# One more channel slice of a long convolution inverted by an eight-way split, with the pacing of the work lengthened

## The chip, the cores and the metric

The kernel runs on one core of one Trainium2 chip. The metric is device time in microseconds (us). It computes the output and all gradients of one layer, so it has ten outputs. Engines are named as in the profile: PE is TensorE (matrix products), DVE is VectorE, ACT is ScalarE, POOL is GpSimd and SP is SyncE, which here only issues transfers. PEld is the loading of the stationary operand of a matrix product.

## The reference

With S = 2048 rows, D = 1024 channels and F = 3584 hidden columns, the layer computes

```
xn = layernorm(x)
kv = shift_conv4(k) * v                       # four taps along the rows
y  = irfft(rfft(kv, 2S) * rfft(ssm_k, 2S))[:S] + kv * ssm_D
s  = xn * y                                   # long convolution branch
h  = (xn @ w_gate) * (xn @ w_up)
g  = silu(h @ w_down)                         # gated linear branch
out = x + s * g
```

and then the gradients of `out` to x, k, v, the shift taps, `ssm_k`, `ssm_D`, `w_gate`, `w_up` and `w_down`, for a given `grad_out`. The change concerns only how `y` is brought back from the frequency domain for some of its channels.

## The kernel before

The channels of the long convolution are done in eight slices of 128 channels, ds = 0 to 7 (the sixth slice is ds = 5). Each slice is transformed to 16 groups of spectra on 128 partitions, with 256 columns (two halves of the rows for 128 channels). For a slice the order is: forward transform of the filter and of `kv` (lines 771 to 796), product of the spectra (333 to 358), inverse (line 847), and after that its rows (`tail`, 743 to 752). The inverse has a VectorE part that leaves a tile G of 16 groups (a tile named HX in the trace), and a TensorE part, four row groups `rp`, each of which writes one PSUM tile `psY`, is copied to `yf` by ScalarE, and after the fourth is stored to DRAM as `YFd`.

There are two versions of this inverse, and the tuple `INV8` (line 680) says which slices use the second.

- `inv_dft` (367 to 388) and `inv_rows` (441 to 452): the VectorE part stops after two levels of sums and differences, six instructions. Each row residue then needs four matrix products of 128x256, so a slice needs 32.
- `inv8` (395 to 430) and `inv8_rows` (433 to 439): the VectorE part goes one level further, 16 instructions, some of them with the factor C8. Each residue needs two matrix products, so a slice needs 16.

While the convolution runs on VectorE, TensorE does the gate and up products: 14 column slabs of 256 by 16 row blocks, each block eight matrix products 128x512 into `psg` (line 645). After each block a function `tick` counts one and lets the convolution, a Python generator, emit more instructions. Each `yield` carries a weight in us; `F_TOTAL` (859 to 861) is the sum of the weights, and each tick lets the generator go on until its done weight reaches

```
(SHIFT_W + (F_TOTAL - SHIFT_W) * (cnt[0] + 6.5) / (NT + 3.5))        # line 923, NT at line 916
```

where `cnt` is the tick's number. The weights are of VectorE time less 0.95 of the TensorE time that the convolution adds (`net`, line 244). A tick is a quarter of a unit: a unit is one call of `gu_unit`, four row blocks of one slab. The VectorE multiplication that makes `hN` of a unit (line 659) is emitted at the next unit's first block, and is transposed on TensorE five blocks later (line 674).

After the last block (cnt = 195) comes the down product of the gated branch, in pairs of row blocks: a pair is 28 column chunks of four matrix products 128x512 into two PSUM tiles `psbm` (line 968), so 112 for a pair. The first pair (`bm_first`) still ticks, after every second chunk, so that cnt ends at 209. Then `drain` (line 1260) emits what is left of the convolution, PSUM and SBUF rooms of the convolution are given back, and from there the seven other pairs follow, each block with its `gate` (1197 to 1235): ScalarE copies `psbm` to `bm`, and VectorE computes output and gradients of the gate from `bm`, `x_t`, `do_t`, `xn_t` and `yf_t`. The last is read from `YFd`, all slices at once. The three PSUM accumulators of this phase (`psbm`: two in `ps_bm`, one in `ps_bx`) come free with the copy to `bm`, and the third and fourth blocks of the phase use `ps_bx` and then the first block's own accumulator again.

The instructions of an engine are put in order at build time by a planner with its own model of durations: of the instructions that its model holds to be ready it takes the one that stands first in the program. VectorE instructions of the convolution are pinned in program order (lines 207 to 213); matrix products of the rows (line 438 and 449) are not. In the finished program every engine runs its list strictly in order.

Of the kernel before, what the change touches and what calls it, by code (L numbers as in the profile page):

```python
# [19 lines left out]
def build_kernel(  # L20
# [433 lines left out]
    def by_res(t, rp):  # L454

        return t.rearrange("p (c r) d -> p r c d", c=2)[:, 2 * rp:2 * rp + 2]

    def rowps(ps):
        return ps[:].rearrange("p r (c d) -> p r c d", c=2)
# [217 lines left out]

    h_out = []
    EIGHT = ((0, 0), (0, 1), (7, 0), (7, 1))
    INV8 = (2, 4, 6, 7)  # L680
    SHIFT_W = 8 * 2.3

    conv_state = {"forward": True, "filters": True}
# [1 line left out]
    def conv_forward():  # L685
# [54 lines left out]
        def kvs(ds):  # L740
            return S_["kvt", ds // 2][:, :, ds % 2 * P:(ds % 2 + 1) * P]

        def tail(ds):
            G = S_.pop(("G", ds))
            yf = cs.tile([P, NB, P], BF16, name="yf")
            for rp in range(4):
                ps = (inv8_rows if ds in INV8 else inv_rows)(G, ps_y, rp)
                pe_us[0] += 0.45 if ds in INV8 else 0.9
                nc.scalar.copy(out=by_res(yf[:], rp), in_=rowps(ps))
# [14 lines left out]
        def half(ds, x, i, first=None):  # L764
            if (ds, int(first is not None)) not in EIGHT:
                return fwd4_half(x, i, cf, ps_cv, first)
            SP = cf.tile([P, 2, 2, 512], F32, name="SP", bufs=2)
            fwd8_half(x, i, SP, ps_cv, first, True)
            return SP
# [36 lines left out]
        for ds in range(8):  # L806
# [37 lines left out]
            def ahead():  # L844
                if ds < 7:
                    sp.append(half(ds + 1, kvs(ds + 1), len(sp)))
            yield from (inv8 if ds in INV8 else inv_dft)(KX, HX, cs, ahead if ds % 2 == 0 else None, ahead)
            if ds % 2 == 1:
# [11 lines left out]
    F_TOTAL += len(EIGHT) * (FWD8_W - 9.6 + 0.95 * 1.75) - 2.0  # L860
    F_TOTAL += len(INV8) * (INV8_W - INV_W + 0.95 * 1.8)
    conv = conv_forward()
# [50 lines left out]
    ps_cv = pool("ps_cv", 2, space=PSUM)  # L913
    pump, drain = make_pump(conv, F_TOTAL)
    cnt = [-5]
    NT = 24 * 8.0 + 20

    def tick(by=1):
        cnt[0] += by
# [2 lines left out]
        if cnt[0] >= -2:  # L922
            pump((SHIFT_W + (F_TOTAL - SHIFT_W) * (cnt[0] + 6.5) / (NT + 3.5)) / F_TOTAL)

# [648 lines left out]
def kernel(  # L1573
# [22 lines left out]
    out_9: bass.AP,  # L1596
):
    build_kernel(
        ctx, tc,
        A_q, A_k, A_v, A_shift_k, A_ssm_k, A_ssm_D, B_x, B_w_gate, B_w_up, B_w_down, grad_out,  # L1600
# [32 lines left out]
```

## Time and profile before

| | us |
|---|---|
| median of three runs (1922.61 to 1923.16) | 1922.94 |
| the profiled execution's own time | 1922.53 |
| span of the profiled execution, first to last instruction | 1920.8 |
| gate and up products, roughly | 9 to 513 |
| first pair of the down product | 513 to 539 |
| other seven pairs | 539 to 711 |
| PE busy in the span | 1902.7 |
| DVE busy in the span | 1548.5 |

The profile lists each engine's busy time; windows of it give busy time for a stretch, and the timeline gives instructions in order, with equal neighbours merged (an "x4" at the end is four instructions) and, in brackets, the idle time before them and what ended it. The chain of waits is what led to the last instruction, followed backwards; the list of waits says which engine sat idle for whom. Matrix products overlap in the records: one of 128x256 is shown as 272 ns long, while eight in a row take 0.87 us.

### The profile page before, as it was taken

How to read it: one execution, taken by the hardware profiler on the slowest of the kernel's cores; microseconds unless marked ns; L12 is line 12 of the kernel's file. 1: busy time of each engine (PE TensorE's matmuls, PEld its weight loads, DVE VectorE, ACT ScalarE, POOL GpSimd, SP SyncE). 2: the span in 40 equal slices, each digit the busy share in tenths (PEclk: the TensorE clock that was granted, in tenths of full speed). 3: DMA queues.
4: the chain of work that ended last, by engine and by line, in shares of the span. 5: the costliest groups of instructions: out<-in, count | busy, mean ns of one | idle time of the engine just before them, and what ended most of it. 6: DMA issues, size and time to landing. Idle time of an engine off the chain costs nothing.

```text
span 1920.8 us, 27294 instructions
## 1 busy us (share of the span) xinstructions
PE 1902.7 (99%) x10828; PEld 1028.9 (54%) x10962; DVE 1548.5 (81%) x1705; ACT 638.9 (33%) x943; POOL 328.7 (17%) x461
## 2 busy tenths in 40 slices
PE   8999999999999999999999999999999999999999
PEld 5555655555444456666666666664444444444444
DVE  8999999999967555887899999999996404288884
ACT  5754655555332233332222222221212102011113
POOL 5121212201112220001031131111212001011111
PEclk9999999999999999999999999999999999999999
DMA  8776867659799988557788698585786999889885
GB/s 297 266 262 218 261 208 233 219 207 295 256 295 318 296 305 242 202 196 239 240 255 266 220 259 263 196 283 166 231 255 168 140 207 222 161 176 195 196 177 167
DMA packets 451360, 444.43 MB, mean 231 GB/s; under 512 B 268800, under 2 KB 371612, under 8 KB 436768
## 3 DMA queue, kind: packets, MB, share of 16 engines
q1 hardware_dynamic: 394848, 243.36, 48.3%
q0 software_dynamic: 40064, 169.95, 27.7%
q10 hardware_dynamic: 16320, 29.36, 4.1%
q8 instruction: 86, 1.41, 0.3%
q14 instruction: 42, 0.34, 0.1%
HBM read 194.00 MB, written 185.64 MB: 198 GB/s over the span
## 4 chain that ended last, share of the span: by engine, by line
PE 82%; DVE 7%; issue 4%; DMA 4%; ACT 2%; SPq 0%; POOL 0%; DVEq 0%; ACTq 0%; POOLq 0%
PE psb L1341 20%; PE psg L645 19%; PE psb L1324 10%; PE psbm L968 10%; PE psb L1419 9%; PE psx L1471 6%; PE psF L235 3%; DVE dkp L1179 2%; DMA dkT<-DKSHd 1%; PE tr L674 1%; DVE dxn L213 1%; PE psY L438 1%; PE psY L1127 1%; DMA dkh<-DKSHd 1%; PE psx L1419 1%
## 5 line engine op out<-in xcount | busy, mean ns | idle before, releaser
L645 PE MATMUL psg<-wslab,U 128*128 128x512 bf16 x1734 | 401.7, 379 | 6.1 <-DMA wslab<-in_B_w_gate_dram 2.4
L1341 PE MATMUL psb<-U,U 128*128 128x512 bf16 x1792 | 397.1, 379 | 0.0
L1471 PE MATMUL psx<-U,dgut 128*128 128x512 bf16 x1505 | 331.0, 379 | 1.6
L1471 PEld LDWEIGHTS <-dgut 128*128 128x128 bf16 x1792 | 175.3, 98 | 211.4
L1341 PEld LDWEIGHTS <-U 128*128 128x128 bf16 x1792 | 175.2, 98 | 198.0
L645 PEld LDWEIGHTS <-U 128*128 128x128 bf16 x1792 | 172.4, 98 | 187.9 <-issue 2.5
L1324 PE MATMUL psb<-wdt,U 128*128 128x256 bf16 x1792 | 205.6, 273 | 0.0
L1324 PEld LDWEIGHTS <-U 128*128 128x128 bf16 x1792 | 175.3, 98 | 29.2
L213 DVE TENSOR_TENSOR W<-W 128x1024 f32<-128x1024 f32 (+1 forms) x180 | 177.7, 1004 | 3.9
L1419 PE MATMUL psb<-U,U 128*128 128x512 bf16 x797 | 175.9, 379 | 0.9
L1346 ACT CAST wb<-psb 128x512 bf16<-128x512 f32 x112 | 65.6, 586 | 315.4 <-PE psb L1341 313.4
L968 PE MATMUL psbm<-U,ht 128*128 128x512 bf16 x658 | 144.8, 379 | 0.7
L1419 PEld LDWEIGHTS <-U 128*128 128x128 bf16 x896 | 87.5, 98 | 104.5
L647 ACT CAST gut<-psg 128x512 bf16<-128x512 f32 x156 | 91.4, 587 | 123.7 <-PE psg L645 118.3
L1503 ACT ACTIVATE dx_t<-dxn 128x1024 bf16<-128x1024 f32 x15 | 15.9, 1057 | 326.9 <-DVE dxn L213 326.9
L1179 DVE SCALAR_TENSOR_TENSOR dkp<-dkT,kT 128x1024 bf16<-128x1024 bf16 (+2 forms) x64 | 78.4, 1224 | 41.1 <-DMA dkT<-DKSHd 39.4
L968 PEld LDWEIGHTS <-ht 128*128 128x128 bf16 x672 | 65.7, 98 | 78.6
L213 DVE TENSOR_TENSOR U<-U,dht 128x2048 bf16<-128x2048 bf16 x56 | 68.3, 1221 | 46.2 <-ACT dht L1326 46.1
L1326 ACT CAST dht<-psb 128x512 bf16<-128x512 f32 x112 | 65.6, 587 | 116.4 <-PE psb L1324 115.2
L66 POOL DMA_DIRECT2D Hd<-hN x54 | 36.7, 679 | 294.3 <-DVE hN L213 291.2
L213 DVE TENSOR_TENSOR dxn<-psx,dxna_t 128x1024 f32<-128x1024 f32 x15 | 18.3, 1222 | 77.1 <-PE psx L1471 73.1
L1450 ACT CAST wbs<-psb 128x512 bf16<-128x512 f32 x51 | 29.9, 586 | 145.1 <-PE psb L1419 131.2
(237 smaller groups left out, 2446.5 us busy)
## 6 DMA issues: line engine op xcount, KB each, us to landing
U<-GUd SPq DMA_DIRECT2D x28, 1024.0 KB, 7.2
DGd<-U SPq DMA_DIRECT2D x28, 1024.0 KB, 6.6
GUd<-gut ACTq DMA_DIRECT2D x39, 512.0 KB, 6.4
out_dram<-wb SPq DMA_DIRECT2D x112, 128.0 KB, 4.2
U<-Hd SPq DMA_DIRECT2D x14, 1024.0 KB, 6.5
Hd<-hN POOLq DMA_DIRECT2D x54, 256.0 KB, 4.3
HTd<-hT SPq DMA_DIRECT2D x52, 256.0 KB, 3.6
ht<-HTd SPq DMA_DIRECT2D x6, 1536.0 KB, 11.4
```

Of the source, the lines that this page charges most:

```text
L213: pinned(V.tensor_tensor(o, a, b, op))
L235: mm = nc.tensor.matmul(ps[:, k].rearrange("p (c d) -> p c d", c=2), T[:, r, k, :], xr[:, r], start=(n == 0), stop=(n == len(rs) - 1 and ( ...
L645: gu_mm[0] = nc.tensor.matmul(ps[:], XNT[q][:, dc, qi * P:(qi + 1) * P], w[:, dc].rearrange("p a f -> p (a f)"), start=(dc == 0), stop=(dc ...
L647: nc.scalar.copy(out=gut[:, :, i], in_=ps[:].rearrange("p (a f) -> p a f", a=2))
L968: mm = nc.tensor.matmul(ps[:, dh * 512:(dh + 1) * 512], ht(fc)[:, i * P:(i + 1) * P], WD[fc // 4][:, fc % 4, dh * 512:(dh + 1) * 512], sta ...
L1179: ins = V.scalar_tensor_tensor(prod[:].rearrange("p r d -> p (r d)")[:, lo:H], dkT[:, 0, lo:H], 1.0, kT[:, 0, 13 + m + lo:13 + m + H], op0 ...
L1324: nc.tensor.matmul(ps[:, x * SLW:(x + 1) * SLW], DBMT[2 * hf + g][:, dc, (b % 4) * P:(b % 4 + 1) * P], wdt[:, dc, :], start=(dc == 0), sto ...
L1326: nc.scalar.copy(out=dht[:, 2 * e:2 * e + 2].rearrange("p b f -> p (b f)"), in_=ps[:])
L1341: nc.tensor.matmul(ps[:], XN[b // 4][:, b % 4, dc * P:(dc + 1) * P], dgus[b // 8][:, :, b % 8], start=(b == 0), stop=(b == NB - 1))
L1346: nc.scalar.copy(out=wb[:, dc % 2].rearrange("p a f -> p (a f)"), in_=ps[:])
L1419: nc.tensor.matmul(ps, h[:, f, b, :], DBM[b // 4][:, b % 4, dh * 512:(dh + 1) * 512], start=(b == 0), stop=(b == NB - 1))
L1471: nc.tensor.matmul(ps[:, dh * 512:(dh + 1) * 512], t[n][:, f, i * P:(i + 1) * P], WGU[n][:, f, dh * 512:(dh + 1) * 512], start=(n == 0 and ...
```

## The change

The tuple `INV8` gains slice 5, so its inverse goes by `inv8` and `inv8_rows` where it went by `inv_dft` and `inv_rows`. `F_TOTAL` follows `len(INV8)`. `NT` is longer by five ticks, while the number of ticks that are really made is not changed.

```diff
-    INV8 = (2, 4, 6, 7)
+    INV8 = (2, 4, 5, 6, 7)
 ...
-    NT = 24 * 8.0 + 20
+    NT = 24 * 8.0 + 25
```

Where the tuple is used: line 747 (which row products), 748 (their TensorE weight, 0.45 for 0.9), 847 (which inverse) and 861 (the sum of weights).

## The prediction

> **What bounds the kernel now.** First the page's busy line, then windows, then who waited for whom. PE is busy for 1902.7 of 1920.8 us. In the stage of the convolution DVE is just as full (19.8 of 20 us), up to 535 us; then it has room. The list of waits of PE from 60 to 700 us has two entries of 0.2 us: nothing holds PE in that time.
>
> ```profile
> PE 1902.7 (99%) x10828; PEld 1028.9 (54%) x10962; DVE 1548.5 (81%) x1705; ACT 638.9 (33%) x943; POOL 328.7 (17%) x461
> ```
> ```profile
> 400.00:420.00 20.00, 19.89 (x119) 10.96 (x119) 19.83 (x13) 10.02 (x15) 1.90 (x3) 1.00 0.68 233
> ...
> 500.00:520.00 20.00, 19.87 (x115) 9.98 (x116) 19.76 (x23) 8.26 (x12) 3.58 (x5) 1.00 0.91 295
> 520.00:540.00 20.00, 19.89 (x96) 9.44 (x97) 15.55 (x16) 1.08 (x3) 0.00 (x0) 1.00 0.90 258
> 540.00:560.00 20.00, 19.89 (x96) 9.47 (x97) 9.94 (x17) 9.88 (x11) 3.68 (x5) 1.00 0.88 245
> ```
> ```profile
> PE psF L235 <- ACT SP L295: 0.2, 1, 0.2
> PE psF L235 <- ACT SP L257: 0.2, 1, 0.2
> ```
>
> (The windows' columns are stretch, length, PE, PEld, DVE, ACT, POOL, clock, DMA share, GB/s.) Now the places of the change: in the chain, a row group of the sixth slice (x8) and of the seventh (x4); in the timeline, the VectorE inverse of the sixth slice, then of the eighth, and what PE and DVE do after it.
>
> ```profile
> 431.85 0.87 PE psY L449 x8
> ...
> 488.07 0.44 PE psY L438 x4
> ```
> ```profile
> 410.83 2.28 DVE L213 TENSOR_TENSOR W<-KX 128x2048 f32<-128x2048 bf16 x1
> 413.03 0.69 DVE L213 TENSOR_TENSOR hN<-U 128x1024 bf16<-128x1024 bf16 x1
> 413.63 2.35 DVE L213 TENSOR_TENSOR HX<-W 128x1024 bf16<-128x1024 f32 x2
> ...
> 420.63 0.68 DVE L213 TENSOR_TENSOR hN<-gut 128x1024 bf16<-128x1024 bf16 x1
> ```
> ```profile
> 516.87 0.68 DVE L213 TENSOR_TENSOR hN<-gut 128x1024 bf16<-128x1024 bf16 x1
> ...
> 519.86 2.29 DVE L213 TENSOR_TENSOR W<-KX 128x2048 f32<-128x2048 bf16 x1
> ...
> 533.29 2.50 DVE L283 SCALAR_TENSOR_TENSOR HX<-W 128x512 bf16<-128x512 f32 x4
> 536.77 0.53 PEld L438 LDWEIGHTS <-TI 128*128 128x128 bf16 x4
> 537.31 1.50 PEld L968 LDWEIGHTS <-U 128*128 128x128 bf16 x8
> 538.93 0.53 PEld L438 LDWEIGHTS <-TI 128*128 128x128 bf16 x4
> 539.47 0.64 PEld L968 LDWEIGHTS <-U 128*128 128x128 bf16 x4
> ...
> 546.28 0.69 DVE L213 TENSOR_TENSOR gg<-bm,sig 128x1024 bf16<-128x1024 bf16 x1 [10.49 <-ACT sig L1211]
> ```
>
> The eighth slice's G is complete at 535.79. Its first row group runs 1 us later, after 104 of the first pair's 112 weight loads (16 and 5 and 83 in this view); DVE then stands idle for 10.49 us.
>
> **PE, removed.** Sixteen matrix products 128x256. A row group takes 0.87 us by `inv_rows` and 0.44 by `inv8_rows`; four groups: 4 x 0.43 = 1.7 us. PE waits for nothing here, so this lies on the path: -1.7 us. The copies to `yf` and the store of `YFd` stay as they are. [...]
>
> **DVE, added.** The sixth slice's inverse ran from 410.83 to 420.63, less one `hN` in between (0.60 from start to start): 9.20 us. The eighth slice's, by the longer version, ran undisturbed from 519.86 to 535.79: 15.93. So +6.73 us, on an engine that has no idle time until 535.8. All of the convolution behind it comes 6.7 us later on DVE, and the eighth G is complete at 535.79 + 6.73 = 542.5. What takes this up is the idle 10.49 us before the first gate, and the seven gates behind, which need some 6.8 us of DVE for 12.1 us of PE each.
>
> **The pace.** `F_TOTAL` is 413.5 and gains 6.8 + 0.95 x 1.8 = 8.5, so 422.0. Per tick that is (413.5 - 18.4) / 215.5 = 1.833 before and (422.0 - 18.4) / 220.5 = 1.830 after. So up to the sixth inverse nothing moves by more than a tick. Behind it everything is emitted 8.5 / 1.83, say five ticks later against PE's blocks: 5 x 1.73 us plus 1.25 transposes of `hN` at 0.45, less the 1.7 saved, 7.5 us. DVE moves by 6.7 plus 1.25 `hN` at 0.60, also 7.5. So DVE's small lag behind the emission (0.6 to 3.6 us) stays, and with it the absence of PE waits up to 511 us. Costs nothing; if the lag grew, PE would wait for it one for one.
>
> **The moved rows.** Ticks end at 209: the pump stops at 215.5 / 220.5 and leaves 5 x 1.83 = 9.2 weight units; the convolution ends with 1.5 (last piece of the inverse), 3.0 and four times 1.0. So this piece and all four row groups come out of `drain`, behind all 112 products of the first pair. Those end at 538.9 before; without 1.7 and without the row group that stood ahead (0.44) PE is there at 536.8. G comes at 542.5. If the planner knows that, it fills the 5.8 us with some 26 products of the second pair, as it did with four between the last row groups, and the wait is 0. If it thinks G ready at once, PE waits 5.8 us. The trace has no such place; the nearest rows are the two early waits of PE for a normalised row of DVE, 0.8 and 0.7 us after some 8 to 10 us of unbroken DVE work: the plan ran 7 to 10% ahead of DVE. The chain from the last `hN` to G is 27.8 us (12 of product, 15.9 of inverse): 1.9 to 2.8 us. I take the low side, 2.0 us, since those rows are of short instructions and this chain of long ones; ends 0 and 5.8.
>
> **Queues behind the rows.** The last row group ends near 547, not 542.2. ACT: the copy to `bm` of the first block came right behind the fourth `yf` copy (542.86), so now near 548.7; its accumulator is wanted when the fourth block begins, 536.8 + 12.1 + 1.7 = 550.6 or later: 1.9 us spare, so nothing. POOL stores `YFd` (then idle for 24.7 us; behind it only gate stores). SP waits for that store (5.0 us) with `yf_t`, and behind it are the second gate's loads and the fourth pair's left operand `ht`, issued at 551.5, now 557; it takes 12.8 us to land and is wanted near 585: 15 us spare. Gates 1 to 4 come 5 to 6 us later and catch up. POOL's `KFd`, `HFd` and filter loads move with DVE; they run a slice ahead.
>
> The sum, against the profiled 1922.53: -1.7 + 2.0 = +0.3. The median is 0.4 above that execution, so **1923.2 us**: no change that a measurement tells (a bound of 0.2%, 3.8 us).
>
> **The rivals.** *Full wait, slower.* Row group one stands straight behind the 112, PE waits for G until 542.5. For it: the product order is fixed at build time, and the plan was ahead of DVE in both early waits. Against: it filled the gaps between the last row groups rightly. Price -1.7 + 5.8 = +4.1, 1927.0; it turns the sign beyond 1.7 us of wait, and passes 0.2% beyond 5.5.
> *No wait.* The second pair fills the whole time: 1922.9 - 1.7 = 1921.2. For it: G's delay is plain arithmetic that a model with right durations sees; against: the same early waits.
> *DVE sets the end.* If gates or transposes of `hN` hung on DVE, its 6.7 us would come through: 1922.9 + 6.7 = 1929.6. For it 19.8 of 20 us; against: no PE wait for DVE, 10.49 us idle right behind.
> *Accumulators.* The spare 1.9 us at the first `bm` copy is used up, say by a planner that puts the rows 5 us too late: +3.1 - 1.7, 1924.3, more if the next copies follow late.
> *The change does less than it says:* too few units would be left for `drain`; then rows still stand inside the first pair, G is later than them, and PE waits as in the first rival.
>
> **How the numbers follow.** Part wait (1 to 3.5 us: 1922.2 to 1924.7) 0.42; no wait (under 1: 1921.2 to 1922.2) 0.22; full wait (1924.7 to 1927.0) 0.20, a third of it beyond 0.2%; DVE through 0.08; accumulators and replanned order behind them 0.04, to 1929; better than the saving (a stall of the crowded place near 425 us gone too) 0.04. The range 1920.6 to 1927.6 leaves out the DVE case, part of the last two: 0.15. Slower by over 0.2%: 0.07 + 0.08 + 0.04, 0.19; faster by over 0.2%: 0.04; the rest, 0.77, within.
>
> **What would show it.** `psY` of line 449 at 96, of line 438 at 80 in the forward part. DVE's sixth inverse near 16 us; the eighth ends near 542.5. All four last row groups behind 112 weight loads of line 968; the number in between and PE's idle time before the first tell the rivals apart. First `bm` copy near 549, `yf_t` near 558. PE's other stages shift by one constant. It is wrong if PE waits before 511 us, or if a wait of 2 us or more stands at a gate's accumulator.

## The result and the profile after

The changed kernel takes 1929.17 us (median of seven, 1927.59 to 1930.26); the kernel before, on the same chip, 1922.94. The ratio is 1.0028 with a 95% interval of 1.0019 to 1.0038: slower by 0.2 to 0.4%, against a forecast of no change. The profiled execution took 1929.12 us, 6.59 more than the one of before.

Where the 6.59 us lie was read by comparing, in the two traces, the start of the n-th weight load of the gate and up products and of the down product:

| place | after minus before, us |
|---|---|
| first gate and up product | +0.55 (+0.43 by 410 us) |
| 449 us, behind the sixth slice's rows | -1.29 |
| 482 us | +2.97 |
| 513 us, start of the down product | +4.82 |
| 557 us, behind the last rows | +6.55 |
| from there to the end | +6.55, constant |

So the saving is there in full (-1.72 from 410 to 449 us), then 6.11 are lost between 449 and 513 us, and 1.74 at the last rows. The +0.43 stands from the first product on, before any convolution: it is no part of the change. (The rise from 482 to 513 us is no loss of its own: the gate and up products stand in another order among the convolution's, and PE waits for nothing there.)

First the granted clock, by windows of the kernel after (columns: stretch, length, PE, PEld, DVE, ACT, POOL, clock, DMA share, GB/s):

```profile
450.00:460.00 10.00, 9.45 (x56) 4.73 (x55) 9.86 (x10) 3.63 (x6) 0.67 (x1) 1.00 1.08 353
470.00:475.00 5.00, 2.93 (x18) 1.60 (x17) 4.69 (x3) 0.34 (x1) 0.00 (x0) 1.00 0.82 285
475.00:480.00 5.00, 3.79 (x10) 1.37 (x10) 1.48 (x3) 3.69 (x6) 0.50 (x1) 0.66 0.67 188
540.00:560.00 20.00, 18.59 (x95) 9.04 (x93) 9.50 (x12) 7.55 (x9) 1.15 (x1) 1.00 0.78 206
```

and the same three crowded windows of the kernel before:

```profile
450.00:460.00 10.00, 9.95 (x57) 5.18 (x57) 9.86 (x10) 5.72 (x9) 0.67 (x1) 1.00 0.98 316
470.00:475.00 5.00, 4.95 (x25) 2.29 (x24) 4.96 (x7) 2.09 (x4) 0.67 (x1) 1.00 0.66 183
475.00:480.00 5.00, 5.00 (x40) 3.30 (x38) 4.97 (x7) 4.72 (x7) 0.67 (x1) 1.00 0.96 317
```

PE lost 2 us in 470 to 475, and in the next 5 us it ran ten products where 40, some of them shorter, ran before, at a granted clock of 0.66. ScalarE was busy for 0.34 of the 5 us from 470. The windows at 450 and 540 show the smaller losses: 9.45 of 10 us, and 18.59 of 20. The lists of waits of the kernel after, of PE from 60 to 720 us and of ScalarE from 430 to 520 us (total, times, longest), name the two places and their cause:

```profile
PE psg L645 <- ACT gut L647: 4.1, 2, 3.3
PE psY L438 <- DVE HX L283: 1.3, 1, 1.3
```
```profile
ACT hT L675 <- DMA HTd<-hT: 5.9, 1, 5.9
ACT gut L647 <- DMA GUd<-gut: 3.4, 1, 3.4
```

The last line belongs to the smaller loss at 459 us: a store of `gut` that landed after 10.6 us (8.0 in the kernel before). ScalarE's wait for the store of `hT` was 0.75 us in the kernel before:

```profile
470.76 1.01 ACT L675 COPY hT<-tr 128x1024 bf16<-128x1024 bf16 x1 [0.75 <-DMA HTd<-hT]
```

The timeline of the kernel after shows the chain in order: ScalarE's copy to `hT` cannot start until an older `hT` has been stored; the copy of `psg` to `gut` is queued behind it; PE has no free `psg` until then; and when PE goes on, its weight loads are 0.43 us apart (0.15 + 0.28) where they are 0.216 elsewhere.

```profile
474.66 1.01 ACT L675 COPY hT<-tr 128x1024 bf16<-128x1024 bf16 x1 [5.88 <-DMA HTd<-hT]
475.57 0.59 ACT L647 CAST gut<-psg 128x512 bf16<-128x512 f32 x1
...
476.21 5.30 PE L645 MATMUL psg<-wslab,U 128*128 128x512 bf16 x16 [3.28 <-ACT gut L647]
...
476.99 0.15 PEld L645 LDWEIGHTS <-U 128*128 128x128 bf16 x1 [0.28 <-issue]
```

The distances between weight loads give the size: one of 0.99 us (459.23) and one of 3.66 (472.55) where 0.22 is normal, and behind the second seven of 0.43 between one of 0.35 and one of 0.29, which are 1.7 us more than nine of 0.216: 0.77 + 3.44 + 1.7 = 5.9 of the 6.1 us.

The store came late because of what was queued then. This is the issue of transfers by SP and by POOL, after

```profile
448.22 0.37 SPq L540 DMA_DIRECT2D wslab<-in_B_w_up_dram  x1
448.65 2.60 SPq L540 DMA_DIRECT2D wslab<-in_B_w_gate_dram  x1
451.43 5.16 SPq L61 DMA_DIRECT2D U<-in_B_w_down_dram  x2
456.75 0.39 SPq L61 DMA_DIRECT2D U<-HTd  x1
457.24 18.81 SPq L61 DMA_DIRECT2D HTd<-hT  x3
...
449.37 0.56 POOL L66 DMA_DIRECT2D HFd<-HX  x1 [4.03 <-DVE HX L213]
```

and before:

```profile
449.51 0.37 SPq L540 DMA_DIRECT2D wslab<-in_B_w_up_dram  x1
449.93 0.57 SPq L540 DMA_DIRECT2D wslab<-in_B_w_gate_dram  x1
450.69 2.89 SPq L61 DMA_DIRECT2D U<-in_B_w_down_dram  x2
453.74 0.90 SPq L61 DMA_DIRECT2D U<-HTd  x1
454.75 17.40 SPq L61 DMA_DIRECT2D HTd<-hT  x3
...
441.90 0.55 POOL L66 DMA_DIRECT2D HFd<-HX  x1 [3.98 <-DVE HX L213]
```

The last weight slabs, two loads of the down weights (1 MB each) and the first load of transposed `h` (1 MB, a `U<-HTd`) go out on SP within 9 us (5 in the kernel before), and the 256 KB store of `hT` stands behind them: it landed at 470.68 before and at 474.58 after. In the kernel before, the seventh slice's store to `HFd`, 1 MB on POOL, had landed at 447.21, ahead of all this. Now VectorE's work is 7.5 us later, the store is issued at 449.37 and moves in the middle of it (landed 459.0). So the store of `hT` lands 3.9 us later by the clock (2.5 of them because SP comes to it later, held longer by its own issues of the loads, 2.60 and 5.16 us where 0.57 and 2.89 stood), and PE's program stands 1.3 us earlier than before: 3.9 + 1.3 = 5.2, and ScalarE's wait grew by 5.88 - 0.75 = 5.13.

At the last rows, the timeline of the kernel after:

```profile
543.52 0.38 PE L438 MATMUL psY<-HX,TI 128*128 128x256 bf16 x2
543.74 0.81 PE L968 MATMUL psbm<-U,U 128*128 128x512 bf16 x3
545.15 2.50 DVE L283 SCALAR_TENSOR_TENSOR HX<-W 128x512 bf16<-128x512 f32 x4
545.89 0.27 PE L438 MATMUL psY<-HX,TI 128*128 128x256 bf16 x1 [1.34 <-DVE HX L283]
546.00 1.02 PE L968 MATMUL psbm<-U,U 128*128 128x512 bf16 x4
...
551.79 1.02 ACT L1210 CAST bm<-psbm 128x1024 bf16<-128x1024 f32 x1
```

All 112 products of the first pair are in front; two row products run on the half of G that is ready, three products of the second pair follow, and then PE waits 1.34 us, and 0.35 once more before the fourth row product.

### The profile page after: what moved, and what is told of

Read it like the earlier page. It is cut to its first block, busy times and chain, and to the rows that moved or that the text cites. A ratio compares the mean times of both kernels' runs of the same rounds, so it can differ in the third digit from the quotient of the medians.

```text
span 1927.3 us, 27409 instructions
## 1 busy us (share of the span) xinstructions
PE 1910.5 (99%) x10946; PEld 1027.7 (53%) x10946; DVE 1554.9 (81%) x1715; ACT 638.9 (33%) x943; POOL 330.1 (17%) x461
## 4 chain that ended last, share of the span: by engine, by line
PE 94%; DVE 2%; DMA 2%; ACT 1%; issue 0%; SPq 0%; ACTq 0%
PE psb L1341 20%; PE psx L1471 20%; PE psg L645 18%; PE psb L1324 10%; PE psb L1419 9%; PE psbm L968 9%; PE psF L235 3%; PE psY L438 1%; PE tr L674 1%; DMA HTd<-hT 1%; PE psY L1127 1%; PE psx L1419 1%; DVE W L213 1%; PE psY L449 1%; DVE bst L561 0%; DMA wslab<-in_B_w_gate_dram 0%
## 5 line engine op out<-in xcount | busy, mean ns | idle before, releaser
L645 PE MATMUL psg<-wslab,U 128*128 128x512 bf16 x1792 | 409.5, 380 | 7.3 <-ACT gut L647 4.6
L213 DVE TENSOR_TENSOR W<-W 128x1024 f32<-128x1024 f32 (+1 forms) x186 | 183.9, 1005 | 3.9
L1503 ACT ACTIVATE dx_t<-dxn 128x1024 bf16<-128x1024 f32 x15 | 15.9, 1057 | 321.8 <-DVE dxn L213 317.9
```

The source lines that it names most:

```text
L213: pinned(V.tensor_tensor(o, a, b, op))
L645: gu_mm[0] = nc.tensor.matmul(ps[:], XNT[q][:, dc, qi * P:(qi + 1) * P], w[:, dc].rearrange("p a f -> p (a f)"), start=(dc == 0), stop=(dc ...
```

## The experiments

Two theories stood against each other. CROWD: the stores of the convolution, shifted with VectorE, fall into the burst of loads and delay the store of `hT`. LEAD: PE, with 1.7 us less to do, merely arrives earlier at a place that the DMA queues pace. All ratios are to the kernel before, timed beside each (its medians there are 1922.66 to 1923.03 us); a ratio is taken over the executions, late ones too, and is not the quotient of two medians. Each run has one profiled execution, and what is said of waits is read from that one.

**One store left out.** The changed kernel without the seventh slice's store to `HFd`. It leaves that spectrum out: the backward part reads the sixth slice's in its place.

```diff
-            st(HFd[ds], HX[:])
+            if ds != 6:
+                st(HFd[ds], HX[:])
 ...
-                cld(Bs[n], units[n][2][units[n][1]])
+                cld(Bs[n], HFd[5] if n == 6 else units[n][2][units[n][1]])
```

> The changed kernel, but the spectrum of slice 7 (ds = 6) is not stored to HFd, and the backward convolution reads slice 6's in its place; one store of 1 MB, which the change moved from 441.9 to 449.4 us, is taken out. Theory CROWD (the convolution's stores moved into the burst of slab, down-weight and HT loads, so the store of hT lands late and ScalarE blocks): the wait of ScalarE for HTd falls from 5.9 us to under 3.5, PE's wait for gut from 4.6 us to under 1.5, no dip of the clock; 1923.5 to 1925.5. Theory LEAD (PE comes to the burst 1.7 us earlier and only runs into it): the waits stay within 1 us of what they are, 1927 to 1930.

Measured: 1924.57 us (1923.85 to 1927.72), ratio 1.0002 (0.9991 to 1.0013). Some 4.6 of the 6.2 us are gone with one 1 MB store. The store of `hT` landed at 471.10, 3.5 us earlier; the waits, PE's first, ScalarE's second:

```profile
PE psg L645 <- ACT gut L647: 1.6, 2, 1.2
```
```profile
ACT hT L675 <- DMA HTd<-hT: 3.8, 1, 3.8
```

The waits are a little over the bounds given, the time is within its own, and the clock stayed at 1.00. The store of `gut` of 459 us landed after 7.75 us instead of 10.6, and ScalarE did not wait for it. At the burst PE still lost 2.0 of the 6.1 us: the store of `hT` landed only 0.4 us later than in the kernel before, but ScalarE was ready for it 2.6 us earlier. This part goes to LEAD, or to the convolution's other stores, which moved as before (`YFd` is issued at 443.59, at 436.78 in the kernel before); the run does not separate these.

**The store added to the kernel before.** A second store of the same tile, 1 MB, into a room that nobody reads, put behind the `Hd` store at 447 us.

```diff
+    HF2d = dram.tile([P, 16, 256], BF16, name="HF2d")
 ...
+            for n, w in enumerate(product(KX, HX, KX, cs, False, 0)):
+                if (ds, n) == (6, 3):
+                    tc.keep_in_program_order(st(HF2d, HX[:]))
+                yield w
```

> The kernel before, with a second store of slice 7's spectrum (1 MB, to a room nobody reads), held on POOL's queue behind the store of hN that went at 447.0 us; nothing else changes. CROWD: the store of hT issued at about 455 lands 3 us later, ScalarE waits 3 to 5 us for it instead of 0.75, PE waits for gut by 1.5 to 4 us, with the dip of the clock where the wait is over 3; 1925 to 1930. If bytes in the burst are not the cause: no wait, 1922.5 to 1923.5.

Measured: 1925.16 us (1924.59 to 1931.22), ratio 1.0012 (1.0003 to 1.0021).

```profile
447.49 0.64 POOL L66 DMA_DIRECT2D HF2d<-HX  x1
```
```profile
PE psg L646 <- ACT gut L648: 2.0, 1, 2.0
```

The store of `hT` landed 2.9 us later than before, ScalarE's wait grew by as much (0.75 to 3.7), PE waited 2.0 us, and from 482 us to the end everything stands 2.11 us later. The clock was 1.00 from 465 to 480 us. The dip that was expected behind a wait of over 3 us is what the changed kernel had shown (3.28 us of wait, a clock of 0.66 from 475 to 480 us); the wait here was shorter, and 3 us is no bound, for `halfrows` below has a dip behind 2.09. Nothing else differs, so this is the price of 1 MB in that place, with no lead at all. Taken together, roughly: 2.1 for the 1 MB alone, 2.0 that stay without it and 1.7 at half pace are 5.8 of the 6.1 us; the three come from different kernels, so this makes the split likely and does not prove it.

**The saving alone, in the kernel before.** The sixth slice's row products are halved without the longer VectorE part; this leaves out half of the sum for that slice's rows.

```diff
-    def inv_rows(G, psp, rp):
+    def inv_rows(G, psp, rp, js=2):
 ...
-            for j in range(2):
+            for j in range(js):
 ...
-                                     start=(n == 0), stop=(n == 3))
+                                     start=(n == 0), stop=(n == 2 * js - 1))
 ...
-                ps = (inv8_rows if ds in INV8 else inv_rows)(G, ps_y, rp)
+                ps = inv8_rows(G, ps_y, rp) if ds in INV8 else inv_rows(G, ps_y, rp, 1 if ds == 5 else 2)
```

> The kernel before, with only half of the matrix products of the sixth slice's rows (so y of that slice is incomplete): PE is spared the same 16 products, VectorE and all stores stay where they were. CROWD: the saving of 1.7 us comes through nearly whole, 1921.2 to 1922. LEAD: PE waits at the burst by what it came early, and 1922.5 to 1928.

Measured: 1922.07 us (1921.45 to 1928.24), ratio 0.9994 (0.9981 to 1.0008). Six of ten executions lie at 1921.4 to 1922.2, near the saving; four lie above 1926. The profiled one is among these, and its trace has two places: a wait of 1.8 us for `gut` at 473 us, the same chain (ScalarE waited 3.6 us for the store of `hT`, which landed at 473.24), and one far away, in the backward part, where PE's products wait for a load of `dgut` and then run at a lowered clock:

```profile
1655.08 10.28 PE L1471 MATMUL psx<-U,dgut 128*128 128x512 bf16 x39 [2.09 <-DMA dgut<-DGd]
```
```profile
1655.00:1660.00 5.00, 4.92 (x15) 1.92 (x16) 0.00 (x0) 0.00 (x0) 0.00 (x0) 0.66 1.15 309
```

That second place cost 3.9 us by the weight loads and lies far from what the edit touches. The first is no proof of LEAD: this execution began 1.5 us late, so PE came to the burst only 0.25 us earlier by the clock than in the kernel before. It was the store that was slow, 17.7 us where 15.9 stood, although `HFd` had landed at 449.54, ahead of the loads of the down weights. What held the store there is open; this stall came without the 1 MB in the burst. In the median the saving is kept, so PE's lead is not the 6 us.

**The lag alone, in the kernel before.** `NT` longer by five, `INV8` as it was: the whole convolution is emitted later per tick, and PE is given nothing.

```diff
-    NT = 24 * 8.0 + 20
+    NT = 24 * 8.0 + 25
```

> The kernel before with NT longer by five ticks alone: everything is emitted up to five ticks later, no work changes. CROWD: the stores of slice 6 and 7 come some 3.7 ticks (6.8 us) later at the burst, as in the change, so PE waits there for gut by 2 to 5 us; with a wait or none at the last rows 1925 to 1930. LEAD: no PE saving, so no wait at the burst; 1922.5 to 1924.

Measured: 1933.15 us (1930.07 to 1939.89), ratio 1.0049 (1.0032 to 1.0067), above the range given. `HFd` is issued at 447.60 in place of 441.90, the store of `hT` lands at 474.83, and (PE from 60 to 1900 us, then ScalarE):

```profile
PE psg L645 <- ACT gut L647: 5.2, 1, 5.2
PE psx L1471 <- DMA dgut<-DGd: 3.1, 1, 3.1
PE psY L438 <- DVE HX L283: 1.7, 2, 0.9
```
```profile
ACT hT L675 <- DMA HTd<-hT: 6.0, 1, 6.0
```

Both losses of the changed kernel are here without its saving, 6.9 us at the burst with the half pace behind it and 2.0 at the last rows, and PE comes to the burst no earlier than in the kernel before (0.01 us). So delaying the convolution by some ticks is enough, without any lead. The profiled execution took 13.8 us more than that of the kernel before; a further 4.7 of these are the wait for a load of `dgut` at 1656 us, the place that `halfrows` showed, and half pace behind it.

**The split alone.** The changed `INV8` with the old `NT`.

```diff
-    NT = 24 * 8.0 + 25
+    NT = 24 * 8.0 + 20
```

> The sixth slice by eight with the old NT: the convolution is emitted 2% faster per tick. CROWD: VectorE is full either way and its work is 6.7 us longer, so the stores come about as late as in the change and PE waits at the burst by 2 to 5 us; 1925 to 1931. If instead the faster pace keeps the stores ahead of the burst, no wait there and under 1923.

Measured: 1927.79 us (1926.88 to 1929.39), ratio 1.0021 (1.0011 to 1.0031). The time is as expected, the place is not: no wait for `gut`, and 1.1 us for the store of `hT`. Instead PE waits for the convolution, from 60 to 720 us:

```profile
PE psF L235 <- ACT SP L257: 3.7, 3, 2.4
PE tr L674 <- DVE hN L213: 1.3, 1, 1.3
PE psF L235 <- ACT SP L295: 0.9, 2, 0.6
```

With 8.5 more weight units over the old number of ticks each tick lets go 1.87 units where VectorE did 1.83: the emission runs ahead of VectorE, and PE pays. So the five ticks do what the pace needs. That the burst costs nothing here is not for an earlier store: `HFd` goes out at 447.98 and the store of `hT` lands at 473.56, 1.0 us before that of the changed kernel. But PE has lost so much by then that it and SP's loads come 3.9 us later than in the changed kernel, and the wait at the burst is exchanged for those on the way to it.

**The burst spread out.** In the changed kernel, the `U<-HTd` load and the second load of the down weights go one and two units later, each behind a store of `hT` in SP's queue.

```diff
-            ld(HTd[b0 // 8][sl // 12][fr:fr + SLW, so:so + n * P].rearrange("(a f) s -> f a s", f=P),
+            ht_st[0] = ld(HTd[b0 // 8][sl // 12][fr:fr + SLW, so:so + n * P].rearrange("(a f) s -> f a s", f=P),
 ...
-        load_wd(1)
-        ld(HT0[0], ht_rows(0, 0, 16))
 ...
+                if (hf, sl) == (0, NSL - 2):
+                    with tc.issue_after(ht_st[0].ins):
+                        load_wd(1) if b0 else ld(HT0[0], ht_rows(0, 0, 16))
```

> The changed kernel, with the loads of HT0 (1 MB) and of the second block of the down weight (1 MB) taken out of the burst and issued one and two units later, each behind a store of hT. CROWD: the store of hT has only 1 MB ahead of it on SP's queue, ScalarE's wait for HTd falls from 5.9 us to under 1, PE's wait for gut to under 1, no dip of the clock; the wait of 1.3 at the last rows stays: 1922 to 1924.5. If the wait has another cause it stays, 1927 to 1930.

Measured: 1924.06 us (1923.27 to 1929.15), ratio 1.0008 (1.0 to 1.0017). `HFd` still goes out at 448.92, in the same company; but the store of `hT` no longer stands behind 3 MB. It is issued at 452.81, behind one load of 1 MB, and lands at 466.32; ScalarE waits for no store of `hT`:

```profile
451.16 1.47 SPq L61 DMA_DIRECT2D U<-in_B_w_down_dram  x1
452.81 3.48 SPq L61 DMA_DIRECT2D HTd<-hT  x1
456.45 0.47 SPq L61 DMA_DIRECT2D U<-HTd  x1
```

PE's two largest waits that are left (the second is behind the store of `gut`, which here takes 11.0 us):

```profile
PE psY L438 <- DVE HX L283: 1.3, 1, 1.3
PE psg L645 <- ACT gut L647: 1.2, 1, 1.2
```

So what costs is the store's place in SP's queue, together with the crowd, and not VectorE, which is as late here as in the changed kernel. (The edit puts the store ahead of 2 MB and also thins the burst; the run does not say which of the two gave how much.) The same edit in the kernel before:

> The same loads moved in the kernel before. CROWD: it stood at the edge (0.75 us of wait on ScalarE, PE's wait hidden), so the median hardly moves, 1922.0 to 1923.2, but its own late runs of 1926 to 1929 us go.

Measured: 1923.82 us (1922.53 to 1930.91), ratio 1.0008 (0.9997 to 1.0018). Nothing is gained, and the late executions of the kernel before (17 of 93 in all lay over 1926 us) did not go away. That expectation was wrong: they need not come from the burst at all. The wait for `dgut` above, in `halfrows` and `ntonly`, is one other place; which the kernel before has when it is late is open, since none of its late executions was profiled.

**Covering the last rows.** As `spread`, with thirteen column chunks of the second pair's first block written ahead of the last four row groups.

```diff
+    HELD = 13
 ...
+    ps2 = ps_bx.tile([P, D], F32, name="psbm")
+    for fc in range(HELD):
+        bm_mm(ps2, ht1[0], 0, fc)
     drain()
 ...
-            ps = (ps_bx if (2 * bp + i) % 3 == 2 else ps_bm).tile([P, D], F32, name="psbm")
-            for fc in range(NF):
+            ps = ps2 if (bp, i) == (1, 0) else (ps_bx if (2 * bp + i) % 3 == 2 else ps_bm).tile([P, D], F32, name="psbm")
+            for fc in range(HELD if (bp, i) == (1, 0) else 0, NF):
```

> spread, and the last four row groups emitted behind 13 of the 28 chunks of the second pair's first block. If both waits of the changed kernel are named rightly, neither is left and the 1.7 us of the sixteen products remain: 1920.8 to 1922.2, 1 to 2 us under the kernel before. If holding the rows makes the first gate's copy or the fourth block late, PE waits there and it is 1922.5 to 1926.

Measured: 1924.09 us (1921.76 to 1935.17), ratio 1.0015 (1.0 to 1.003). The wait at the rows is gone and PE stands 0.72 us ahead of the kernel before up to 696 us, but in the profiled execution (1929.95) a new one follows in the tail of the gates:

```profile
PE tr L1234 <- DVE dbm L213: 6.1, 1, 6.1
```
```profile
678.11 14.57 SPq L1279 DMA_TRANSPOSE U<-DBMd  x1
```

SP held that transpose for 14.57 us (5.98 in the kernel before), and the loads of the last gates came behind it. Five of twelve executions lie below 1923.5, four above 1929.9. Why the transpose is held in some was not settled.

**Fewer held.** The same with three chunks (`held3`), and that once more with the first load of the down weights behind a store of `hT`, the `U<-HTd` load behind the next and the second load of the down weights after these (`held3w`).

```diff
-    HELD = 13
+    HELD = 3
```

and for `held3w` also, against `held3`:

```diff
-    with tc.issue_after(slab_ld.ins):
-        load_wd(0)
 ...
         if hf == 1:
+            load_wd(1)
             load_wd(2)
 ...
-                        load_wd(1) if b0 else ld(HT0[0], ht_rows(0, 0, 16))
+                        ld(HT0[0], ht_rows(0, 0, 16)) if b0 else load_wd(0)
```

> This is `spread` with three column chunks of the second pair's first block (12 products, 2.6 us) put ahead of the last row groups, where `both` held thirteen. What remains in `spread` is 1.3 us of waiting plus 0.4 at the rows and 1.2 us behind a store of `gut`, together 1.8 over the kernel before by the shift. CROWD: the wait at the rows (1.3 us) goes and nothing behind the rows moves by more than 1 us, so `yf_t` comes as in `spread`; shift at the end +0.1 to +0.9, median 1922.3 to 1923.5, no difference to the kernel before. LEAD, by which the time lost is that of a PE that arrives early anywhere: the wait moves to the next place that hangs on VectorE or a load, and the median stays at 1924. If the late values of `both` (over 1929) come from the products held back and not from their number, some runs here are also above 1928.

Measured: 1925.29 us (1923.39 to 1928.29), ratio 1.0 (0.9987 to 1.0013). The wait did not go, it was cut in two:

```profile
PE psY L438 <- DVE HX L283: 1.4, 2, 0.7
```

The expectation's size was wrong: a chunk of one block is two products, so three chunks are six, 1.3 us and not 2.6. By the weight loads all six ran ahead of the first row product and one more ahead of the fourth; in `spread` three and four stood between the row products, seven as well. So as much stood in front of the fourth row product as in `spread`, and this run is no test of the cover.

> As `held3`, with the first two loads of the down weights also put behind the stores of hT, two units later than they are (the first goes out near 461 us, the second with the third, near 470). CROWD: the store of `gut` at 448 that landed after 11 us then lands within 8, ScalarE's wait for it falls from 3.8 to under 1 us and PE's 1.2 us go; shift at the end -1.3 to -0.3, median 1921.3 to 1922.5, the first version below the kernel before, by less than 0.1%. If the queue is only made to bunch later, a wait for a store of `gut` or hT of over 3 us stands between 465 and 490 us instead and the median is 1923 or more.

Measured: 1924.25 us (1923.59 to 1931.72), ratio 1.0004 (0.9992 to 1.0016). The expectation missed at the `gut` store as well: it landed 10.6 us after its issue (448.58 to 459.17), and ScalarE's copy still stood 3.4 us:

```profile
459.27 1.07 ACT L647 CAST gut<-psg 128x512 bf16<-128x512 f32 x2 [3.37 <-PE tr L674]
```

The view names PE's transposes because they ended last, at 459.18, 0.01 us behind the landing. The first load of the down weights went out at 453.47, not near 461, so this edit hardly moved it. PE's wait for `gut` is 0.7 where it was 1.1, and the time is as it was. Of the versions with the changed `INV8`, only `nohf6` had the `gut` store land within 8 us. No version tried that computes the whole result is faster than the kernel before.

## Why the prediction was wrong

- **The saving on PE (-1.7)** was right: -1.72 between 410 and 449 us. PEld was busy for only 54% of the kernel before, and still PE had no slack there: in that kernel's gate and up products the weight loads for 512 columns stood 0.216 us apart, in the row groups of the same stage those for 256 columns 0.109, and from 60 to 720 us PE waited twice, 0.2 us each.
- **VectorE's addition (+6.73)** was right: the sixth inverse runs from 411.18 to 428.66 with three `hN` in between, 15.7 us. The eighth G is complete at 547.65; that is 5.1 us behind the 542.5 of the working, near the 4.8 by which the whole program stood later by then.
- **The pace ("costs nothing", no PE waits up to 511 us)** fell: PE waits at 459 and 473 us. The arithmetic itself held, VectorE kept its lag (PE waited for no convolution before the last rows, and with the old `NT` it did). What was not asked is what else is in the machine at the moment to which the shift of 7.5 us moves the work.
- **The step that failed** is the sentence "POOL's `KFd`, `HFd` and filter loads move with DVE; they run a slice ahead", costed at nothing. It speaks of who reads them, and that is beside the point: what matters is whom they delay. One of them, 1 MB, moves into the burst of SP's loads, and the last in SP's queue is a 256 KB store that ScalarE and, behind it, PE wait for. The loss at the burst was 6.1 us in the profiled execution where the working had nothing; without that one store the median came back by 4.6 us, and the store alone, added to the kernel before, cost 2.1.
- **The lowered clock** was not in the working: of the 6.1 us, 1.7 are products at half pace behind the wait (weight loads 0.43 us apart where 0.216 is normal, a clock of 0.66 from 475 to 480 us).
- **The wait at the moved rows (2.0, between 0 and 5.8)** was right in kind and nearly in size: 1.34 + 0.35. That its size came out by way of a plan 7 to 10% ahead of VectorE is not shown, so the nearness may be luck. What the trace shows is that neither end was met: the planner put seven products of the second pair in front, 1.5 us, and the four products of the first row group ran as the parts of G came (two, one, one), all of them begun before G was complete at 547.65. PE did not have to wait for the whole of G, as the upper end supposed.
- **The queues behind the rows** held: the first copy to `bm` starts at 551.79 (near 549 expected, plus what was lost), `yf_t` is issued at 557.58, no accumulator is waited for, and PE's shift is constant from 557 us to the end.
- **The rivals.** The rival that VectorE sets the end gave 1929.6, which is the time measured, by another way: VectorE's 6.7 us did not come through to PE, and `spread` has the same 6.7 us with a time of 1924.06. No rival named a transfer, and the range ended below the result for that reason.

With the terms that the run showed, -1.72 + 1.74 + 6.11 is +6.1, and the 0.4 of the start make 6.6. The first two are near the working's -1.7 and +2.0; the third is the one it left out.

## What to carry to other kernels

When an edit shifts a stretch of work by some us, list every transfer that it issues and look, at the new time, at what the other queues have under way and who waits for the last of it. Here the reader of the moved transfer was not the one who paid: it was a small store (256 KB, landed after 17.3 us) behind large loads in one queue, and moving the loads behind the store (`spread`) brought back 5.1 of the 6.2 us. A saving of 1.7 us is soon spent: here 5.1 us were lost at a place where ScalarE's wait had been 0.75 us and PE had waited for nothing.

## What the runs showed of the hardware

- A 256 KB store on SP, issued 0.5 us behind a 1 MB load with 2 MB and a slab still in flight, took 17.3 us to land (457.24 to 474.58). In `spread` the same store, issued at 452.81 behind one load of 1 MB, took 13.5 us. The store of `hT` before it, ahead of the burst, took 5.3 us in the changed kernel and 5.2 in `spread`.
- The granted clock fell behind some short idle times and not behind others. Distances between weight loads of 2.68 us (`halfrows`, the late load of `dgut`), 3.66 (the changed kernel), 3.70 and 5.61 (`ntonly`) and 6.66 (`both`) were each followed by products at half pace for some 3 to 4 us, weight loads of 512 columns 0.43 us apart (a clock of 0.66 from 475 to 480 us in the changed kernel and from 1655 to 1660 in `halfrows`, 0.82 from 480 to 485 in `ntonly`, 0.50 from 710 to 715 in `both`). Distances of 1.54 (`nohf6`), 2.21 (`halfrows`), 2.37 (`extra`) and 2.77 (`nt20`) were not (1.00 from 470 to 485 us in `halfrows` and from 465 to 480 in `extra`; the mean clock of `nohf6` and `nt20` was 1.0); behind the last the loads stand 0.11 us apart, as they do for 256 columns in the row groups at full pace. The 2.68 us had half pace behind it and the longer 2.77 had not: in these two runs the length of the idle time alone did not decide it.

```profile
430.82 1.95 PE L235 MATMUL psF<-hx,TF 128*128 128x256 bf16 x16 [2.39 <-ACT SP L257]
```

- In the changed kernel the mean clock was 1.000 in two of seven executions, which took 1927.6 us, and 0.998 or 0.999 in the others, which took 1929.1 to 1930.3. The profiled one, with its 1.7 us at half pace, is of the second kind; that the two of the first had no half pace is read from their clock alone.
